# Reordering the opening of a fused Fourier-mixing and hardswish kernel: where raw weights wait, when the second stage starts, who sums x

## The chip, the cores and the metric

The kernel runs on one core of one Trainium2 chip. The metric is the device time of the whole kernel in microseconds (us); before the change its median over three runs is 2004.42 us. The engines are named as in the profile: PE is TensorE (PEld its weight loads), DVE is VectorE, ACT is ScalarE, POOL is GpSimd and SP is SyncE, which here only issues transfers.

## The reference

The first part takes the real part of a two-dimensional Fourier transform of x, over the 3008 sequence positions and the 256 features, for each of 8 batch entries. The result, as 24064 tokens of 256 features, goes through two matrix products with a hardswish between them.

```python
def _attn_ref(x):                      # x: (8, 3008, 256) float32
    X = np.fft.fft(x, axis=1)
    X = np.fft.fft(X, axis=2)
    return X.real.astype(np.float32)

def _moe_ref(x, w_in, w_out):          # x: (24064, 256); w_in: (256, 2048); w_out: (2048, 256), both float64
    h = x @ w_in
    relu6 = np.clip(h + 3.0, 0.0, 6.0)
    g = h * relu6 / 6.0
    return (g @ w_out).astype(np.float32)
```

Both weights are float64: they arrive as 8-byte words and the kernel makes float32 of them itself.

## The kernel before: the opening

The sequence transform is split as 3008 = 47 x 64. Batch entries are taken in four pairs. For the first pair, x arrives in eight parts (`c`); each part is folded (mirrored halves summed) and multiplied by the stage-one table F; the result z goes to DRAM and comes back rearranged as g, on which stage two works with the table T. The feature transform is folded into the weights: `fold_w_in` multiplies w_in by the matrix C. Then come the steps: `mlp1` is the first matrix product with its hardswish, `combine` sums gated values on GpSimd, and `mlp2` is the second product in seven terms instead of eight. There are 384 such steps. Only the opening, up to the first steps, is touched by the change.

The weights come in 16 raw pieces of 512 KB. Pieces 0 to 3 and 6 to 9 belong to w_in, 4, 5 and 10 to 15 to w_out. A piece passes through five operations:

```python
def load_w(j):                                   # GpSimd requests the transfer
    st = wpool.tile([P, 2 * WB], I32, tag="st", bufs=4, name="st")
    ...                                          # nc.gpsimd.dma_start(...)
def exponent_a(j):                               # ScalarE, two passes (L457)
    for i in range(2):
        nc.scalar.activation(low, top, AF.Identity, bias=bias[:, i:i + 1], ...)
def exponent_b(j):                               # TensorE, two matmuls (L462)
    ex = ps_h.tile([P, WB], F32, tag="uv", name="ex")
    ...
def exponent_c(j):                               # ScalarE (L466)
    nc.scalar.activation(exs[j][:].bitcast(I32), exs[j][:], AF.Identity, scale=2.0 ** 23)
def mantissa(j):                                 # VectorE (L474, L475)
    ...
def join(j):                                     # VectorE: mantissa times exponent (L483 or L490)
    ...
```

Two pieces make a pair. A pair of w_in goes through `fold_w_in` (eight TensorE matmuls, L522, into two banks, which ScalarE copies to W1); a pair of w_out goes through `mix_w_out` (four VectorE sums, L509 to L512). The order is set by three functions, in which each engine does its part of piece j and finishes the piece before it:

```python
pending, copies = [], []

def on_scalar(j):
    for i in pending:
        exponent_c(i)
    if j is not None:
        exponent_a(j)
    while copies:
        copies.pop(0)()

def on_vector(j):
    if j is not None:
        mantissa(j)
    for i in pending:
        join(i)

def on_tensor(j):
    if j is not None:
        exponent_b(j)
    done = pending.pop() if pending else 0
    if done % 2:
        use_pair(done // 2)                      # fold_w_in or mix_w_out
    if j is not None:
        pending.append(j)

for c in range(NXC):                             # the eight parts of x
    if c + 2 < NXC:
        load_x(first, c + 2)
    load_w(c + 2)
    if c < NXC - 1:
        fold_first(first, c)                     # half the sums on VectorE, half by accumulation on TensorE
    else:
        for part in range(2):
            fold(first, c, part, nc.vector)      # all sums on VectorE
    on_scalar(c)
    on_vector(c)
    for i in range(XC // 2):
        (stage1_first if c < NXC - 1 else stage1)(first, c, i)
    on_tensor(c)
    if c == 0:
        load_t(0)
    ...
load_g(first, 0)
for j in range(NXC, 15):
    if j < 14:
        load_w(j + 2)
    on_scalar(j)
    on_vector(j)
    keep_awake(1)                                # idle matmuls
    on_tensor(j)
...
keep_awake(2)
for i in range(2):
    stage2(first, 0, i)
spread(first, 0)
...
on_scalar(15)
on_vector(15)
mlp1(*chunk(0))
mlp1(*chunk(1))
on_tensor(15)
combine(*chunk(0))
```

Tiles take their space from pools by tag: `a` (4 buffers) and `c` (3) serve the steps later, and parts of x of the first pair lie in them during the opening. The PSUM tag `uv` has three buffers, shared by `ex`, the idle matmuls and the two halves u and v of `mlp1`. `stage1_first` runs 16 matmul instructions for one part of x, `stage1` half of that work.

Of the kernel before, what the change touches and what calls it, by code (L numbers as in the profile page):

```python
# [8 lines left out]
I32 = mybir.dt.int32  # L9
# [47 lines left out]
def kernel(  # L57
# [10 lines left out]
    nc = tc.nc  # L68
    P = nc.NUM_PARTITIONS
    B, S, D = x.shape  # L70
# [7 lines left out]
    NXC = NS // XC  # L78
# [15 lines left out]
    apool = ctx.enter_context(tc.tile_pool(name="apool", bufs=4))  # L94
    cpool = ctx.enter_context(tc.tile_pool(name="cpool", bufs=3))
# [15 lines left out]
    C = consts.tile([P, 2, D], F32, name="C")  # L111
# [96 lines left out]
    def bank(shape, name):  # L208
        if starting[0]:
            return ps_a.tile(shape, F32, tag="acc", name=name)  # L210
        return ps_d.tile(shape, F32, tag="d", name=name)
# [73 lines left out]
    def spread(pr, gr):  # L285
        pr.qn[gr] = qpool.tile([P, 2 * TB], F32, tag="qn", name="qn")
        if starting[0]:
            ps = bank([P, 2 * TB], "ps3")
            for kk in range(2 * KK):
                nc.tensor.matmul(ps[:, kk * P:(kk + 1) * P], pr.g[gr][:, kk, D:D + 1].to_broadcast([P, P]),  # L290
                                 T[:, :, gr, 1, kk], start=True, stop=True)
            nc.scalar.copy(pr.qn[gr][:], ps[:])
        else:
            qd = dpool.tile([1, 2 * TB], F32, tag="qd", name="qd")
            nc.sync.dma_start(out=qd[:], in_=pr.q[gr][P - 1:P, 1].rearrange("p k n -> p (k n)"))
            nc.sync.dma_start(out=pr.qn[gr][:], in_=qd[:].to_broadcast([P, 2 * TB]))
        del pr.g[gr]
# [120 lines left out]
    first = pairs[0]  # L418

    wctx = tc.tile_pool(name="wpool", bufs=1)  # L420
    wpool = wctx.__enter__()
# [5 lines left out]
    WB = 512  # L427
# [4 lines left out]

    def load_w(j):
        kind, n, i = PIECES[j]
        st = wpool.tile([P, 2 * WB], I32, tag="st", bufs=4, name="st")
        o = st[:].bitcast(moe_w_in.dtype)
        if kind == "in":
            nc.gpsimd.dma_start(out=o, in_=moe_w_in[i * P:(i + 1) * P, n * WB:(n + 1) * WB])
        else:
            r = (2 * n + i * NF) * P  # L440
            nc.gpsimd.dma_start(out=o.rearrange("p (c j) -> p c j", c=2),
                                in_=moe_w_out[r:r + 2 * P, :].rearrange("(c p) d -> p c d", p=P))
        raw[j] = st
# [9 lines left out]
    def exponent_a(j):  # L453
        top = raw[j][:].bitcast(I16).rearrange("p (n four) -> p n four", four=4)[:, :, 3]
        for i in range(2):
            low = PM[:, j % 2, i].bitcast(U8).rearrange("p (n two) -> p n two", two=2)[:, :, 0]
            nc.scalar.activation(low, top, AF.Identity, bias=bias[:, i:i + 1], scale=(1 - 2 * i) / 16.0)  # L457
# [7 lines left out]
    def exponent_c(j):  # L465
        nc.scalar.activation(exs[j][:].bitcast(I32), exs[j][:], AF.Identity, scale=2.0 ** 23)  # L466

    def mantissa(j):
        st = raw.pop(j)
        hi = st[:].rearrange("p (n two) -> p n two", two=2)[:, :, 1]  # L470
        lo = st[:].bitcast(U32).rearrange("p (n two) -> p n two", two=2)[:, :, 0]
        top = wpool.tile([P, WB], I32, tag="top", bufs=2, name="top")
        frac = top[:].bitcast(F32)
        nc.vector.tensor_scalar(top[:], hi, 0xFFFFF, 0x100000, op0=AL.bitwise_and, op1=AL.bitwise_or)  # L474
        nc.vector.scalar_tensor_tensor(frac, lo, 2.0 ** -32, top[:], op0=AL.mult, op1=AL.add)  # L475
        fracs[j] = frac
# [20 lines left out]
    def use_pair(j):  # L497
        kind, n, _ = PIECES[2 * j]
        if kind == "in":
            fold_w_in(n)  # L500
        else:
            mix_w_out(n)
# [11 lines left out]
    def fold_w_in(n):  # L514

        cs = slice(n * WB, (n + 1) * WB)
        ws = [w.pop(("in", n, i)) for i in range(2)]
        sums = []
        for blk in range(2):
            ps = bank([P, WB], "wps")  # L520
            for i in range(2):
                nc.tensor.matmul(ps[:], C[:, i, blk * P:(blk + 1) * P], ws[i], start=(i == 0), stop=(i == 1))  # L522
            sums.append(ps)

        def copy():
            for blk in range(2):
                nc.scalar.copy(W1[:, blk, cs], sums[blk][:])
            nc.sync.dma_start(out=wn[n:n + 1], in_=W1[P - 1:P, 1, cs])

        copies.append(copy)  # L530


    def load_wn(n):
# [3 lines left out]
    def load_t(gr):  # L537
        for b in range(2):
            nc.sync.dma_start(out=T[b * N2:(b + 1) * N2, b, gr], in_=c_stage2[:, gr])


    def keep_awake(n):
        ps = ps_h.tile([P, 2 * TB], F32, tag="uv", name="awake")
        for i in range(n):
            nc.tensor.matmul(ps[:], ones[:], Z[:], start=True, stop=True)
# [1 line left out]
    Z = spool.tile([P, 2 * TB], F32, tag="s", name="Z")  # L547
    nc.vector.memset(Z[:], 0.0)
    nc.vector.memset(ones[:], 1.0)
    keep_awake(6)  # L550
    nc.sync.dma_start(out=F[:], in_=c_stage1)
    bias = wpool.tile([P, 2], F32, tag="bias", name="bias")
    for i in range(2):
# [6 lines left out]
    CE = spool.tile([P, 2, P], F32, tag="s", name="CE")  # L560
    dim = c_dim.rearrange("(h p) d -> p h d", p=P)
    nc.sync.dma_start(out=CE[:], in_=dim[:, :, D:])
    nc.sync.dma_start(out=C[:], in_=dim[:, :, 0:D])
    E = wpool.tile([P, 2, P], F16, tag="E", name="E")
    nc.scalar.copy(E[:], CE[:])
    for b in range(2):
        r = slice((1 - b) * N2, (2 - b) * N2)
        t = T[r, b].rearrange("p g a k n -> p g (a k n)")
# [6 lines left out]
    load_w(0)  # L575
    load_x(first, 1)
    load_w(1)

    pending, copies = [], []

    def on_scalar(j):
        for i in pending:
            exponent_c(i)
        if j is not None:
            exponent_a(j)
        while copies:
            copies.pop(0)()

    def on_vector(j):
        if j is not None:
# [9 lines that stand above are left out]
            use_pair(done // 2)  # L602
        if j is not None:
            pending.append(j)

    for c in range(NXC):
        if c + 2 < NXC:
            load_x(first, c + 2)
        load_w(c + 2)
        if c < NXC - 1:  # L610
            fold_first(first, c)
        else:
            for part in range(2):
                fold(first, c, part, nc.vector)
        on_scalar(c)
        on_vector(c)
        for i in range(XC // 2):
            (stage1_first if c < NXC - 1 else stage1)(first, c, i)
        on_tensor(c)
        if c == 0:  # L620
            load_t(0)
        if c in (4, 6):
            load_wn(PIECES[c - 4][1])
    load_g(first, 0)
    for j in range(NXC, 15):
        if j < 14:
            load_w(j + 2)
        on_scalar(j)
        on_vector(j)
        keep_awake(1)  # L630
        on_tensor(j)
    load_wn(PIECES[6][1])
    load_wn(PIECES[8][1])
    load_g(first, 1)
# [2 lines left out]
    for i in range(2):  # L637
        stage2(first, 0, i)
    spread(first, 0)
    starting[0] = False  # L640


# [3 lines left out]
    after = {}  # L646

    def beside(p):
        at = {}

        def put(t, f, *a):
            at.setdefault(t, []).append((f, a))

        cur = pairs[p]
        if p == 0:
            for f in (on_scalar, on_vector, on_tensor):
                after.setdefault(1, []).append((f, (None,)))
            for gr in range(2, NG):
                after.setdefault(gr, []).append((load_t, (gr,)))
            put(NF - 1, close_w)  # L660

        def s2(t, pr, gr):
            for i in range(2):
                put(t + 3 + 4 * i, stage2, pr, gr, i)
            put(t + 8, spread, pr, gr)

        for gr in range(1, NG):
            if gr > 1:
                put(NST * (gr - 2) + 12, load_g, cur, gr)
            s2(NST * (gr - 1), cur, gr)  # L670
        if p + 1 < NP:
            nx = pairs[p + 1]
            for c in range(NXC):
                put(9 * c, load_x, nx, c)
                put(9 * c + 3, fold, nx, c, 0, nc.gpsimd)
                put(9 * c + 5, fold, nx, c, 1, nc.gpsimd)
                for i in range(XC // 2):
                    put(9 * c + 8 + 3 * i, stage1, nx, c, i)
            put(NST * (NG - 1) - 2, load_g, nx, 0)
            put(NST * (NG - 1) + 8, load_g, nx, 1)  # L680
            s2(NST * (NG - 1), nx, 0)
        return at
# [10 lines left out]
    def chunk(s):  # L693
        p, ck, fc = steps[s]
        return chunks[p][ck], fc

    on_scalar(15)
    on_vector(15)
    mlp1(*chunk(0))
    mlp1(*chunk(1))  # L700
    on_tensor(15)
    combine(*chunk(0))
    prev = None
    for s, (p, ck, fc) in enumerate(steps):
# [96 lines left out]
```

## Time and profile before

| | before |
|---|---|
| median of three runs | 2004.42 us (2000.66 to 2004.54) |
| span of the profiled run, mean granted TensorE clock | 2002.9 us, 0.993 |
| busy: PE, DVE, ACT, POOL | 1965.6, 1437.2, 701.2, 1417.9 us |
| first 82 us: PE, DVE, ACT, POOL busy | 72.0, 45.7, 52.5, 23.4 us |
| first 82 us: DMA share, moved | 0.93, 256 GB/s |

How to read it: the busy times say how long an engine had work, not whether it set the end. A line of the chain gives the start, the duration and what ran. A line of the order of time gives start, duration, engine, line of the kernel, operation, output and input, with the idle time before it and what ended that in brackets. A line of the waits says which group waited for which: us in total, times, longest.

### The profile page before, as it was taken

The page shows a single profiled execution, that of the slowest core. Times are in us where ns is not written, and L with a number is a line of the kernel's source. Part 1 is how long each engine was busy: PE and PEld are TensorE (multiplying, and loading weights), DVE is VectorE, ACT ScalarE, POOL GpSimd, SP SyncE. Part 2 cuts the span into 40 slices and gives each one's busy share as a digit, 9 for nine tenths or more (in the row PEclk, how much of TensorE's full clock was granted, in tenths as well). Part 3 has the DMA queues.
Part 4 walks back from the last instruction along what each step waited for, and adds up shares of the span by engine and source line. Part 5 has one row for each costly group of instructions (what it writes and reads, how often), then busy time and mean ns, then how long its engine had stood idle before and what let it go on. Part 6 is the DMA issues. An engine that isn't in the chain of part 4 may idle for free.

```text
span 2002.9 us, 28366 instructions
## 1 busy us (share of the span) xinstructions
PE 1965.6 (98%) x9178; PEld 1691.5 (84%) x9178; DVE 1437.2 (72%) x2701; ACT 701.2 (35%) x1198; POOL 1417.9 (71%) x1612
## 2 busy tenths in 40 slices
PE   9899999999999999999999999999999999999997
PEld 5488888888888888888888888888888888888886
DVE  5677767776777777776777767777678777777775
ACT  6533333333333333333333333333333333333332
POOL 3277778776777787777658877778666667667665
PEclk9899999999999999999999999999999999999998
DMA  9512211211112122110201221112110101101100
GB/s 275 162 27 59 51 40 48 55 38 35 28 35 51 41 51 56 50 51 25 48 18 30 69 56 39 51 43 53 35 27 20 27 17 27 32 12 27 27 11 19
DMA packets 158985, 93.54 MB, mean 47 GB/s; under 512 B 131019, under 2 KB 143819, under 8 KB 158838
## 3 DMA queue, kind: packets, MB, share of 16 engines
q1 hardware_dynamic: 149366, 58.22, 12.1%
q0 software_dynamic: 9472, 33.49, 6.1%
q8 instruction: 75, 1.23, 0.3%
q14 instruction: 72, 0.59, 0.1%
HBM read 54.32 MB, written 37.33 MB: 46 GB/s over the span
## 4 chain that ended last, share of the span: by engine, by line
PE 93%; DVE 3%; ACT 1%; issue 0%; POOL 0%; DVEq 0%; POOLq 0%; ACTq 0%
PE acc L379 55%; PE v L325 16%; PE u L325 16%; PE ps L280 2%; PE ps L226 2%; DVE a L357 1%; ACT t L354 0%; DVE u L338 0%; DVE s L330 0%; ACT PM L457 0%; PE wps L522 0%; DVE o L405 0%; DVE v L344 0%; DVE u L341 0%; PE ps L223 0%
## 5 line engine op out<-in xcount | busy, mean ns | idle before, releaser
L369 POOL TENSOR_TENSOR c<-a 128x512 f32<-128x512 f32 (+1 forms) x384 | 478.4, 1246 | 454.9 <-PE acc L379 358.1
L379 PE MATMUL acc<-c,G 128*128 128x256 f32 (+1 forms) x3072 | 712.1, 375 | 0.0
L354 ACT ACTIVATE t<-u,half 128x512 f32<-128x512 f32 (+2 forms) x416 | 272.4, 655 | 1104.6 <-DVE u L338 1092.9
L379 PEld LDWEIGHTS acc<-c,G 128*128 128x128 f32 x3072 | 577.5, 190 | 72.7
L330 DVE SCALAR_TENSOR_TENSOR s<-qn,WN,u 128x256 f32<-128x256 f32 x768 | 334.6, 477 | 351.6 <-PE u L325 351.2
L379 PE MATMUL acc<-a,G 128*128 128x256 f32 (+1 forms) x2304 | 551.2, 375 | 0.0
L379 PEld LDWEIGHTS acc<-a,G 128*128 128x128 f32 x2304 | 434.6, 190 | 57.6
L325 PE MATMUL v<-q,W 127*128 127x256 f32 x1536 | 397.7, 381 | 7.7 <-DVE a L357 7.7
L325 PE MATMUL u<-q,W 128*128 128x256 f32 x1536 | 395.4, 380 | 2.5 <-DVE a L357 2.2
L325 PEld LDWEIGHTS u<-q,W 128*128 128x128 f32 x1536 | 287.8, 190 | 59.9 <-issue 15.8
L325 PEld LDWEIGHTS v<-q,W 127*128 127x128 f32 x1536 | 289.7, 190 | 55.6 <-issue 8.2
L357 DVE SCALAR_TENSOR_TENSOR a<-t,u 128x512 f32<-128x512 f32 (+2 forms) x416 | 266.1, 646 | 95.7 <-ACT t L354 90.3
L369 POOL TENSOR_TENSOR c<-c,a 128x256 f32<-128x256 f32 (+1 forms) x384 | 274.7, 715 | 30.1
L369 POOL TENSOR_TENSOR c<-a,c 128x256 f32<-128x256 f32 (+1 forms) x384 | 274.6, 715 | 30.1
L338 DVE TENSOR_TENSOR u<-s,v 128x512 f32<-128x512 f32 (+1 forms) x384 | 263.1, 685 | 41.5 <-DVE s L330 0.9
L354 ACT ACTIVATE t<-v,half 128x512 f32<-128x512 f32 (+1 forms) x384 | 257.1, 670 | 5.8 <-DVE v L344 4.5
L344 DVE TENSOR_TENSOR v<-v,s 128x512 f32<-128x512 f32 (+1 forms) x384 | 257.9, 672 | 1.1
L357 DVE SCALAR_TENSOR_TENSOR a<-t,v 128x512 f32<-128x512 f32 (+1 forms) x416 | 255.4, 620 | 0.5
L369 POOL TENSOR_TENSOR r<-w,e 128x256 f32<-128x256 f32 (+1 forms) x96 | 92.2, 981 | 3.8
L385 ACT ACTIVATE e<-acc 128x512 f32<-128x512 f32 (+1 forms) x192 | 87.0, 543 | 2.9 <-PE acc L379 2.8
L405 DVE STREAM_TRANSPOSE o<-r 128x256 f32<-128x256 f32 (+1 forms) x192 | 72.5, 416 | 6.6 <-POOL r L369 6.4
L238 ACT COPY z<-ps 96x512 f32<-96x512 f32 x64 | 37.2, 581 | 83.5 <-PE ps L226 63.1
(81 smaller groups left out, 754.0 us busy)
## 6 DMA issues: line engine op xcount, KB each, us to landing
out_dram<-o SPq DMA_DIRECT2D x736, 32.0 KB
zd<-z SPq DMA_DIRECT2D x32, 384.0 KB
g<-zd SPq DMA_DIRECT2D x48, 256.0 KB
xt<-in_x_dram POOLq DMA_DIRECT2D x21, 384.0 KB, 4.0
qn<-qd SPq DMA_DIRECT2D x23, 256.0 KB
st<-in_moe_w_in_dram POOLq DMA_DIRECT2D x8, 512.0 KB, 11.8
st<-in_moe_w_out_dram POOLq DMA_DIRECT2D x8, 512.0 KB, 5.7
xt<-in_x_dram POOLq DMA_DIRECT2D x7, 376.0 KB, 3.9
```

The costliest lines, as they stand in the source:

```text
L226: nc.tensor.matmul(ps[0:PZ], F[0:PR, 0:PZ], y[:, 2 * i:2 * i + 2, :], start=True, stop=True)
L280: nc.tensor.matmul(ps[:, blk, 2 * u:2 * u + 2], g[:, kk, blk * (P + 1):blk * (P + 1) + P], T[:, :, gr, blk, kk], start=True, stop=True)
L325: nc.tensor.matmul(ps[:, i], W1[r, blk, f * P:(f + 1) * P], q[r, blk, of:of + KC], start=True, stop=True)
L330: nc.vector.scalar_tensor_tensor(s[:, i].rearrange("p k n -> p (k n)"), qn[:, of * N2:(of + KC) * N2], WN[:, f:f + 1], u[:, i].rearrange(" ...
L338: nc.vector.tensor_tensor(u[:, :, 0:ns], s[:, :, 0:ns], v[:, :, 0:ns], op=AL.add)
L344: nc.vector.tensor_tensor(v[:, :, 0:nm], v[:, :, 0:nm], s[:, :, 0:nm], op=AL.subtract)
L354: nc.scalar.activation(t, h, AF.Relu, bias=half[:], scale=scale)
L357: nc.vector.scalar_tensor_tensor(dst, t, 1.0, h, op0=AL.min, op1=AL.mult)
L369: nc.gpsimd.tensor_tensor(out, in0, in1, op=AL.add)
L379: nc.tensor.matmul(ch.acc[i // 2][:, i % 2, 0:ch.n], G[:, i, fc, :], mv, start=(fc == 0 and i % 2 == 0), stop=(fc == NF - 1), skip_group_c ...
L385: nc.scalar.mul(ch.e[:, k:i + 1, 0:ch.n], ch.acc[i // 2][:, 0:i + 1 - k, 0:ch.n], 1.0 / WS)
L405: nc.vector.transpose(o[:, 0:n // DH, h], ch.r[:, m, h, 0:n].rearrange("p (j i) -> p j i", i=DH))
```

## The change

Five things are moved in the opening; what is computed stays the same.

- Raw pieces 8 to 14 are put into buffers of the pools `a` and `c`, which x has left by then, so that their requests need not wait for the conversion of earlier pieces. All requests are made by the last part of x, behind x itself.
- Parts 2 and 4 of x are summed wholly on VectorE, like the last one, which takes accumulating matmuls from TensorE in the parts where it also does `fold_w_in`.
- On ScalarE the first exponent pass of piece j comes before the last one of piece j-1, and the copies of a folded pair are taken one piece later, so that ScalarE doesn't stand waiting for TensorE.
- Stage two and the spread stand behind piece 12 instead of 14; pieces 13 to 15 are finished between stage two and the first steps.
- The tables C and T are requested later, and the opening has two more idle matmul calls.

```diff
     def load_w(j):
         kind, n, i = PIECES[j]
-        st = wpool.tile([P, 2 * WB], I32, tag="st", bufs=4, name="st")
+
+        pool, tag = (wpool, "st") if j < 8 or j == 15 else (apool, "a") if j < 12 else (cpool, "c")
+        st = pool.tile([P, 2 * WB], I32, tag=tag, bufs=4 if pool is wpool else None, name="st")
...
-        copies.append(copy)
+        copies[-1].append(copy)
...
-    keep_awake(6)
+    keep_awake(8)
...
-    nc.sync.dma_start(out=C[:], in_=dim[:, :, 0:D])
...
-    pending, copies = [], []
+    pending, copies = [], [[], []]

     def on_scalar(j):
+        for copy in copies.pop(0):
+            copy()
+        copies.append([])
+        if j is not None:
+            exponent_a(j)
         for i in pending:
             exponent_c(i)
-        if j is not None:
-            exponent_a(j)
-        while copies:
-            copies.pop(0)()
...
-        load_w(c + 2)
-        if c < NXC - 1:
+        for j in [c + 2] if c < NXC - 2 else range(4 * c - 16, 4 * c - 12):
+            load_w(j)
+        on_pe = c not in (2, 4, NXC - 1)
+        if on_pe:
             fold_first(first, c)
         else:
             for part in range(2):
...
-            (stage1_first if c < NXC - 1 else stage1)(first, c, i)
+            (stage1_first if on_pe else stage1)(first, c, i)
         on_tensor(c)
         if c == 0:
+            nc.sync.dma_start(out=C[:], in_=dim[:, :, 0:D])
+        if c == 3:
             load_t(0)
...
-    for j in range(NXC, 15):
-        if j < 14:
-            load_w(j + 2)
+    for j in range(NXC, 13):
         on_scalar(j)
         on_vector(j)
+        on_tensor(j)
         keep_awake(1)
-        on_tensor(j)
...
     spread(first, 0)
+    on_scalar(13)
+    on_vector(13)
+    on_tensor(13)
     starting[0] = False
...
         if p == 0:
-            for f in (on_scalar, on_vector, on_tensor):
-                after.setdefault(1, []).append((f, (None,)))
+            for t, f, j in ((0, on_scalar, 15), (0, on_vector, 15), (1, on_tensor, 15),
+                            (2, on_scalar, None), (2, on_vector, None), (2, on_tensor, None)):
+                after.setdefault(t, []).append((f, (j,)))
...
-    on_scalar(15)
-    on_vector(15)
+    on_scalar(14)
+    on_vector(14)
     mlp1(*chunk(0))
+    on_tensor(14)
     mlp1(*chunk(1))
-    on_tensor(15)
     combine(*chunk(0))
```

## The prediction

> **What bounds the kernel now.** I read the busy times by stage first, since every edit lies in the opening, then the chain of work that ended last for the opening, then the waits, then the order of time around the last part of x. The stages (us, busy time and number of instructions of each engine, TensorE clock, DMA share, GB/s):
>
> ```profile
> 0.00:82.00 82.00, 72.02 (x244) 41.16 (x245) 45.74 (x101) 52.47 (x85) 23.41 (x37) 0.94 0.93 256
> 82.00:112.00 30.00, 24.06 (x103) 19.53 (x102) 23.92 (x41) 9.32 (x15) 16.32 (x17) 0.89 0.11 31
> 112.00:1990.00 1878.00, 1869.48 (x8835) 1630.79 (x8833) 1366.56 (x2557) 639.23 (x1099) 1375.04 (x1555) 1.00 0.15 38
> ```
>
> From 112 us on TensorE is busy 1869.5 of 1878 us: nothing the diff touches is there, and whatever the opening gains or loses moves the end one for one. The prize is bounded too: the first output matmuls (L379) start at 93.67 us in the order of time, so 2% (40 us) would be nearly half of all that precedes them.
>
> The chain between the last stage-one matmuls and the first hidden layer (start, duration, what):
>
> ```profile
> 58.06 3.43 PE wps L522 x8
> 61.49 0.86 PE awake L545 x2
> 62.35 0.45 PE ex L462 x2
> ...
> 63.31 1.41 ACT PM L457 x2
> ...
> 64.77 0.38 PE ex L462
> 65.14 3.43 PE wps L522 x8
> ...
> 76.97 1.72 PE awake L545 x4
> 78.69 1.78 PE ps L280 x16
> 80.47 0.91 PE ps L290 x8
> ```
>
> No DMA stands in it: ScalarE's two exponent passes (PM, 1.41) and TensorE's weight products (wps, 3.43) hand over to each other, about 7.1 us per pair of w_in pieces. The requests for raw weights do wait for their buffers, in the waits of the opening:
>
> ```profile
> POOL st L441 <- ACT PM L457: 15.5, 5, 5.0
> ```
>
> but this is GpSimd's own idle time; pieces 8 to 15 are converted without a single wait for a transfer. While x comes in it is otherwise: VectorE waits for it. Order of time around piece 6 and the last part of x:
>
> ```profile
> 45.77 0.57 ACT L466 ACTIVATE ex<-ex 128x512 int32<-128x512 f32 x1
> 46.06 0.43 DVE L474 TENSOR_SCALAR top<-st 128x512 int32<-128x512 int32 x1 [1.21 <-DMA st<-in_moe_w_in_dram]
> 46.28 1.41 ACT L457 ACTIVATE PM<-st,bias 128x512 uint8<-128x512 int16 x2
> ...
> 47.13 0.75 DVE L490 TENSOR_TENSOR G<-top,ex 128x256 f32<-128x256 f32 x2
> 47.79 0.42 DVE L509 TENSOR_TENSOR G<-G,b 128x256 f32<-128x256 f32 x1
> ...
> 49.38 0.55 DVE L165 TENSOR_TENSOR xt<-xt 94x381 f32<-94x381 f32 x1
> ```
>
> Piece 6 lands at 46.06 us, piece 5 is joined at 47.13, its four sums follow from 47.79, and at 49.38 the fold of the last x starts with no idle time before it. So the landing of piece 6 and VectorE's order set when x is done.
>
> **What the Trainium skill says.** "TensorE: Matmul & The Clock Gate", Part 1: activity is watched in windows of about 3.4 us, an idle one halves the clock. The trace agrees in kind and is harsher: after 2.45 us of idling at 9.16 us the matmuls run at the low clock until about 19.8 us. "DMA: Bandwidth & Descriptors", Queues, rings and completion order: each engine goes round the queues that have work, so weights queued on GpSimd can share time with the writes and reads of z from SyncE; the DMA share of 0.93 over the first 82 us fits, the sharing itself no view shows apart. "GPSIMD Engine Reference", 1. Specifications: VectorE instructions with two SBUF inputs contend with GpSimd. Here the sums of a w_out pair take 0.42 us at 71 us with GpSimd idle, and 0.83 to 1.48 us at 103 to 106 us beside its additions.
>
> **The change part by part.** I lay the new order out with the durations above.
>
> *Buffers and requests.* Pieces 8 to 14 need no longer wait for the conversion of 4 to 10. In the trace pieces 10 to 15 were requested at 47.98, 54.00, 57.93, 60.30, 65.02 and 67.38 us; now all should be out soon after 50. The traffic stays; at the 200 to 300 GB/s of that stretch the last of them (4.2 MB for eight) should land about 67 us, instead of about 73 (67.38 plus the 5.7 of a w_out piece). As nothing on the chain waited for them: 0 us. C behind the first part of x and T behind the fourth move 0.26 MB each about within a stretch in which the DMA engines are full: x arrives some 1 us earlier at first and the same by piece 6: 0 us.
>
> *Two parts of x on VectorE.* It costs 2 x (2 x 0.55 + 0.68 + 0.68 + 0.16 - 1.52) = 2 x 1.1 us of VectorE and saves TensorE half of 3.4 us twice. TensorE did lag by 3 us in the fourth part (x folded at 27, its products from 30.1), but had caught up by the seventh (folded 44.85, products from 45.18). 0 us. Two more keep-awake matmuls fill the gap before 11.6 us; x binds there: 0 us.
>
> *ScalarE's order.* exponent_a(j) now comes before exponent_c(j-1). For piece 6 this hurts: exponent_a waits for the landing at 46.06 and takes 1.42, exponent_c 0.58, so the join of piece 5 starts at 48.1, not 47.13; with the sums the fold of the last x starts about 50.5, not 49.38: **+1.1 us**. Afterwards exponent_a(8) from 56.8, exponent_c(7) to 58.8, join (0.69) to 59.5: the first late wps at 59.5 instead of 57.9, another **+0.5**. From the end of one wps block to the start of the next: copy 0.58 + exponent_a 1.42 + exponent_c 0.58 + join 0.69 + hand-overs 0.25 = 3.5 us; before it was 64.98 - 61.49 = 3.5. The looser order gains nothing there, since the copies now stand ahead of exponent_a.
>
> *Second stage behind piece 12.* From the start of the second wps to stage two: wps 3.43 + copy 0.59 + exponent_a 1.42 + ex 0.4 + three keep-awakes 2.6 + hand-overs 0.2 = 8.6 us; before 78.69 - 64.98 = 13.7: **-5.1**. Stage two starts about 75.1 and the spread row is copied by 78.4 (before 81.98). But two pieces now stand between it and the first hidden layer: exponent_a(13) 1.42, exponent_c(12) 0.58, exponent_a(14) 1.42, exponent_c(13) 0.58, join 0.75 = 4.75 us, where before it took 83.18 - 81.98 = 1.2: **+3.55**. The first s (L330) thus starts at 83.15, as before (83.18).
>
> *Sums in the first steps.* The four sums of the third w_out pair, 4 x 0.42 = 1.7 us, now stand on VectorE between the first and the second mlp1, where TensorE has nothing else and waits for a bank: **+1.65**. Piece 15 moves from before the first mlp1 to steps 0 to 2: 1.1 + 0.75 us and then a join and sums beside GpSimd, about 4 us. VectorE has some 1.15 us to spare per 4.75 us step, and a similar backlog cost 1.55 us at 110 us before: 0.
>
> Sum: +1.1 + 0.5 - 5.1 + 3.55 + 1.65 = **+1.7 us**, so the first mlp2 at about 95.4 us instead of 93.67.
>
> **The rivals.** (a) The weights really were late and the conversion runs ahead: stage two at 70 us, the end at 1996 to 1999. The 15.5 us of waiting requests speak for it; that no conversion after piece 7 waited for a transfer speaks against. (b) The clock. No keep-awake now stands between ex(7) and ex(8), so TensorE has a gap of some 1.4 us after 4 us of idling, and part of the eight wps matmuls may run at the low clock: +1 to +2, 2006 to 2008. (c) With eight weight transfers queued, z of the last part and the rows g for stage two land late. Before, g was requested at 60.4, three us after the last z request; it has until 75 us, and only past that does the end move: 2007 to 2012. The margin of about 5 us speaks against.
>
> **Range and chances.** The laid-out sum gives 2006.1. I shade it by one microsecond to 2005.0: the order of short operations on ScalarE can fall better than I laid it, and the three runs of before reach from 2000.66 to 2004.54 with the median at the top. Each of five terms is uncertain by 1 to 2 us, so 3 to 4 together; with the rivals and the 4 us of spread: 1998 to 2011. More than 40 us either way is out of reach of an opening of 94 us with this DMA traffic: 0.01 faster, 0.98 the same, 0.01 slower.
>
> **What would show it.** Right: the last x folded on VectorE near 50.5; wps blocks near 59.5 and 66.5; stage two (L280) near 75; the first s near 83; four sums of 0.42 between the first two groups of s; the first L379 near 95; no DMA in the chain after 55 us. Wrong: conversion of pieces 8 to 12 ahead of 55 us or faster than 6.9 us per pair, stage two before 72 us, a wait of L280 for g, or a main stage whose 8.5 us of TensorE idling has changed.

## The result, and the profile after

The changed kernel takes 2012.04 us (2011.36 to 2012.93, four runs), the kernel before 2004.47: a ratio of 1.0043, with a 95% interval of 1.0025 to 1.006. That is within 2%, as forecast, but 7.6 us longer by the medians (8.6 by the ratio), outside the range of 1998 to 2011 us and far above the 0.6 us that the 2005.0 amounts to.

The stages of the changed kernel (columns as before: us, busy time and instructions of PE, PEld, DVE, ACT and POOL, TensorE clock, DMA share, GB/s):

```profile
0.00:82.00 82.00, 67.20 (x212) 35.48 (x213) 42.61 (x93) 47.51 (x78) 23.99 (x37) 0.94 0.80 247
82.00:112.00 30.00, 22.16 (x78) 16.79 (x78) 23.52 (x41) 10.85 (x18) 12.20 (x13) 0.77 0.20 56
112.00:1990.00 1878.00, 1869.03 (x8828) 1629.84 (x8827) 1370.69 (x2562) 638.01 (x1096) 1375.61 (x1554) 1.00 0.15 38
```

The main stage is untouched: 1869.0 us of TensorE against 1869.5. The difference lies in the opening, where TensorE has done less work by 82 us (67.2 us against 72.0). A sharper measure is the start of the output products of the fifth step: 115.87 us before, 122.98 us after. From there to the end of the span it is 1887.0 us before (2002.9 - 115.87) and 1886.6 after (2009.6 - 122.98), and between 1886.6 and 1887.0 in every trace of this study. So each traced execution can be judged by that one instant.

The chain of the changed kernel from the last part of x on (start, duration, what):

```profile
54.81 0.46 DVE xt L165
...
63.89 3.67 PE wps L524 x8
...
70.14 3.45 PE wps L524 x8
...
78.88 1.78 PE ps L280 x16
```

Compare with the chain before: stage two (L280) at 78.88 against 78.69, though it now stands behind piece 12 and not 14. What the new order saves has been lost ahead of it: the last part of x is folded from 54.7 us, not 49.4. And between the last weight product and stage two, 5 us shorter as predicted, the chain still has no transfer. The transfer that hurts is earlier. The order of time around the first weight product, TensorE and SyncE:

```profile
16.40 0.58 SPq L625 DMA_DIRECT2D C<-in_c_dim_dram  x1
...
22.73 0.60 PE L464 MATMUL ex<-PM,E 128*128 128x512 f16 x2
...
27.84 6.74 PE L524 MATMUL wps<-wi,C 128*128 128x512 f32 x8 [4.51 <-DMA C<-in_c_dim_dram]
...
34.41 0.60 PE L199 MATMUL ps<-xt,F 94*96 94x258 f32 x2
```

C is requested at 16.40 us and the first product that needs it starts at 27.84, after 4.51 us in which TensorE stood still; the products of the fourth part of x, which was folded at 22.4 us, stand behind it in TensorE's program. Behind the gap the eight matmuls take 6.74 us, and from 28 to 32 us the granted clock is 0.50. In the kernel before, the same line in the order of time has no wait and takes 3.60:

```profile
26.69 3.60 PE L522 MATMUL wps<-wi,C 128*128 128x512 f32 x8
```

So TensorE loses 4.51 + 3.14 = 7.65 us there, and the fourth part of x is multiplied only from 34.41.

The start of landmarks in us, in the two profiles (s is VectorE's first result in an mlp1, L330; the value predicted for the second s follows from its 83.15 and its +1.65):

| | before | after | predicted for after |
|---|---|---|---|
| last x folded (L165) | 49.38 | 54.73 | 50.5 |
| first late weight product | 57.90 | 63.73 | 59.5 |
| second late weight product | 64.98 | 69.98 | 66.5 |
| stage two | 78.53 | 78.72 | 75.1 |
| first s | 83.18 | 86.51 | 83.15 |
| second s | 86.87 | 93.67 | 88.5 |
| first output product | 93.67 | 100.46 | 95.4 |
| output products of the fifth step | 115.87 | 122.98 | - |

Stage by stage the change is +5.35 (to the last fold), +0.48, -0.83, -4.81 (to stage two), +3.14 (to the first s), +3.47 (to the second), -0.01, +0.32: together 7.11 us. Two of these need a cause that the prediction didn't have: the first and the one between the first and the second s.

### The profile page after: what moved, and what is told of

It reads as the page before. It is cut to its first block, busy times and chain, and to the rows that moved or that the text cites. A ratio compares the mean times of both kernels' runs of the same rounds, so it can differ in the third digit from the quotient of the medians.

```text
span 2009.6 us, 28311 instructions
## 1 busy us (share of the span) xinstructions
PE 1964.8 (98%) x9154; PEld 1688.3 (84%) x9154; DVE 1440.3 (72%) x2705; ACT 699.5 (35%) x1198; POOL 1418.8 (71%) x1612
## 4 chain that ended last, share of the span: by engine, by line
PE 92%; DVE 3%; ACT 1%; issue 0%; SPq 0%; DMA 0%; POOL 0%; DVEq 0%; POOLq 0%; ACTq 0%
PE acc L379 55%; PE v L325 16%; PE u L325 16%; PE ps L280 2%; PE ps L226 2%; DVE a L357 1%; ACT t L354 0%; DVE u L338 0%; DVE s L330 0%; PE wps L524 0%; DVE o L405 0%; PE awake L547 0%; SPq L411 0%; DMA out_dram<-o 0%; PE ps L223 0%
## 5 line engine op out<-in xcount | busy, mean ns | idle before, releaser
L330 DVE SCALAR_TENSOR_TENSOR s<-qn,WN,u 128x256 f32<-128x256 f32 x768 | 334.3, 477 | 350.7 <-PE u L325 350.1
```

The costliest lines, as they stand in the source:

```text
L330: nc.vector.scalar_tensor_tensor(s[:, i].rearrange("p k n -> p (k n)"), qn[:, of * N2:(of + KC) * N2], WN[:, f:f + 1], u[:, i].rearrange(" ...
```

## The experiments

Theory: C comes too late, and TensorE carries the loss through the parts of x. Rival: the new order on ScalarE and VectorE makes the last fold late, and C's wait is absorbed. A second question is the sums between the first two mlp1.

Each ratio compares a run with the kernel before on the same chip; it is estimated with its interval and is not the quotient of two medians. Medians of different rows can come from different chips, on which the kernel before itself had medians of 2003.9 to 2005.5 us. Single executions of one kernel spread over up to 10 us here. A trace, and with it the landmarks of a row, is one execution: those of e1, e12 and e9 are 2.7, 2.9 and 4.0 us faster than the medians beside them, those of e5 and e6 2.8 and 4.3 us slower. So the lengths of stages inside a trace are better evidence than its instants.

| run | median us | ratio to before (95%) | last fold | stage two | first s | second s | fifth step |
|---|---|---|---|---|---|---|---|
| after (first timing) | 2012.04 | 1.0043 (1.0025 to 1.006) | 54.73 | 78.72 | 86.51 | 93.67 | 122.98 |
| after_again | 2012.25 | 1.0039 (1.0025 to 1.0053) | 54.21 | 80.21 | 88.00 | 95.16 | 124.46 |
| e1_c_early | 2007.49 | 1.0014 (1.0003 to 1.0024) | 47.49 | 72.08 | 79.87 | 87.03 | 116.34 |
| e12_c_early_again | 2009.39 | 1.0020 (1.001 to 1.003) | 49.25 | 73.84 | 81.63 | 88.79 | 118.09 |
| e2_tables_early | 2008.59 | 1.0019 (1.0011 to 1.0027) | 49.44 | 74.04 | 81.84 | 88.99 | 118.32 |
| e3_before_c_late | 2007.22 | 1.0011 (1.0005 to 1.0018) | 52.97 | 81.59 | 86.25 | 89.93 | 119.47 |
| e4_sums_later | 2011.39 | 1.0032 (1.002 to 1.0045) | 54.94 | 80.98 | 88.77 | 92.45 | 123.74 |
| e5_c_early_sums_later | 2005.68 | 1.0008 (1.0002 to 1.0015) | 52.64 | 77.22 | 85.01 | 88.70 | 119.99 |
| e6_c_early_scalar_old | 2007.53 | 1.0013 (1.0006 to 1.002) | 49.74 | 79.46 | 86.47 | 94.03 | 123.34 |
| e7_c_early_stage_late | 2007.15 | 1.0015 (1.0009 to 1.0022) | 49.01 | 78.04 | 83.99 | 87.68 | 117.91 |
| e8_c_early_buffers_old | 2007.86 | 1.0025 (1.0012 to 1.0037) | 49.04 | 75.56 | 83.34 | 90.50 | 119.61 |
| e9_early13 | 2005.13 | 1.0005 (0.9999 to 1.0012) | 47.51 | 71.44 | 75.69 | 82.06 | 112.45 |
| e10_c_early_fold_pe | 2007.47 | 1.0012 (1.0004 to 1.0019) | 51.24 | 75.83 | 83.63 | 90.79 | 119.71 |
| e11_best | 2002.06 | 0.9988 (0.9979 to 0.9997) | 48.08 | 71.28 | 75.53 | 81.90 | 112.30 |

**C back at its old place.**

```diff
     nc.sync.dma_start(out=CE[:], in_=dim[:, :, D:])
+    nc.sync.dma_start(out=C[:], in_=dim[:, :, 0:D])
...
-        if c == 0:
-            nc.sync.dma_start(out=C[:], in_=dim[:, :, 0:D])
```

> The changed kernel with the request of C back at its old place, before x. Theory (late C): in the changed kernel the first weight product waits 4.5 us for C and then runs 6.7 instead of 3.6 us at a low clock, and TensorE carries these 8 us on to the last part of x. Then here the first weight product starts near 23.5 us and takes about 3.6, the fold of the last part of x starts near 47 instead of 54.7 us, and the whole takes 2003 to 2006 us. Rival (order on ScalarE and VectorE): the last fold is late because exponent_a stands before exponent_c and two parts of x are summed on VectorE; C's wait is absorbed. Then the last fold stays at 53 us or later and the whole at 2010 or more.

Order of time of this run, TensorE:

```profile
23.72 3.60 PE L524 MATMUL wps<-wi,C 128*128 128x512 f32 x8
```

The wait is gone, the product takes 3.60 us, the last fold starts 7.2 us earlier, at 47.49, and the fifth step 6.6 us. The theory's landmarks came as told (23.5, 3.6, 47). The time, 1.0014 of before, was 1.5 us above the upper end expected. Because the two had been timed on different chips, both ran once more side by side:

> The changed kernel once more, beside the version with C early, on one chip. Theory (late C): its first weight product again waits 4 to 5 us for C and runs at the low clock, whatever the arrival of x; its time lies 4 to 6 us above the version with C early. Rival (the difference seen so far came from the arrival of x and the clock, which change from run to run): less than 2 us apart.

> The changed kernel with C back at its old place, once more, beside the changed kernel on one chip. Theory (late C): 4 to 6 us below the changed kernel and 1 to 3 us above the kernel before, which is what the prediction's sum gave without the wait for C. Rival: less than 2 us below the changed kernel.

The changed kernel again shows the gap and the low clock:

```profile
27.96 6.08 PE L524 MATMUL wps<-wi,C 128*128 128x512 f32 x8 [4.33 <-DMA C<-in_c_dim_dram]
```

The medians differ by 2.9 us, the ratios by 0.0019 (3.8 us), the two traces by 6.4 us in the span. Of the 6.4, 3.6 come from where the two traced executions lie beside their medians (2.9 us below and 0.6 above). The time thus falls just short of the 4 to 6 us expected here, and the rival's less than 2 doesn't fit. With the first pair of timings, whose ratios differ by 0.0029 (5.8 us), C's wait is worth 3 to 6 us of the loss; with C early the rest, 3 to 4 us over the kernel before, stays.

**Both tables back.** As above, and `load_t(0)` again behind the first part of x.

> The changed kernel with both tables at their old places: C before x, T behind the first part of x. Theory (late C): C explains the loss, so the time is that of the run with C alone moved back, 2003 to 2006, within 1.5 us of it. Rival (T in the way of x): T early delays x by some 3 to 5 us, as the kernel before shows it against the changed one (fifth part of x at 32.0 against 26.9 us); then this is 2 to 5 us slower than with C alone moved back.

1.1 us above e1_c_early in the median, with overlapping intervals: the times can't be told apart. In the trace x was later (fifth part at 31.0 against 28.5 us), as the rival had it, and the last fold later by 1.95 us; e12, with T late, has its last fold at 49.25 as well, so this one trace doesn't settle T.

**C late in the kernel before.**

```diff
         if c == 0:
+            nc.sync.dma_start(out=C[:], in_=dim[:, :, 0:D])
             load_t(0)
```

(and the request ahead of x taken out)

> The kernel before with one thing of the change alone: C is requested behind the z of the first part of x, together with T. Theory (late C): C lands some 11 us after its request near 18 us, so the first weight product waits from 26.5 to about 29.5 us and may then run at the low clock; the whole takes 2007 to 2011 us. Rival: the kernel before has slack there, and stays within 1.5 us of 2004.5.

```profile
27.97 6.65 PE L522 MATMUL wps<-wi,C 128*128 128x512 f32 x8 [4.60 <-DMA C<-in_c_dim_dram]
```

The same wait and the same slow product appear in the old order, and the last fold moves from 49.4 to 53.0 us. The late request of C is thus enough for both, without the new order. The cost in time is 1.8 us by the medians and 2.2 by the ratio: the theory's 2007 to 2011 meant 2.5 us or more over its 2004.5, so the cost lies between theory and rival, and below the 3 to 6 us that C is worth in the new order.

**The sums behind the second mlp1.**

```diff
     mlp1(*chunk(0))
-    on_tensor(14)
     mlp1(*chunk(1))
+    on_tensor(14)
```

> The changed kernel with piece 14's exponent matmuls and the four sums of the third w_out pair behind the second mlp1 instead of between the first and the second. Theory (sums on the path): the four sums took 3.5 us there, beside GpSimd, and the second group of s waited for them; now it starts about 3.3 us earlier, near 90.3 us, and the whole takes 2008 to 2009.5 us. Rival: the sums only move on, into the start of the third mlp1, and as much is lost there; the whole stays at 2011 or more.

First what is moved: in the changed kernel the order of time between the first two groups of s reads, on VectorE and GpSimd,

```profile
86.51 0.87 DVE L330 SCALAR_TENSOR_TENSOR s<-qn,WN,u 128x256 f32<-128x256 f32 x2
90.19 0.42 DVE L511 TENSOR_TENSOR G<-G,b 128x256 f32<-128x256 f32 x1
90.36 1.37 POOL L369 TENSOR_TENSOR c<-a 128x512 f32<-128x512 f32 x1 [40.31 <-DVE a L357]
90.65 1.37 DVE L512 TENSOR_TENSOR G<-G 128x256 f32<-128x256 f32 x1
91.81 0.79 POOL L369 TENSOR_TENSOR c<-c,a 128x256 f32<-128x256 f32 x1
92.05 0.83 DVE L513 TENSOR_TENSOR G<-G 128x256 f32<-128x256 f32 x1
...
92.80 0.94 DVE L514 TENSOR_TENSOR G<-G,b 128x256 f32<-128x256 f32 x1
93.67 0.86 DVE L330 SCALAR_TENSOR_TENSOR s<-qn,WN,u 128x256 f32<-128x256 f32 x2
```

The first sum runs alone and takes 0.42 us. Then GpSimd begins the first `combine`, and the other three take 1.37, 0.83 and 0.94: 3.5 us from the first sum to the second s, not 1.7. In e4_sums_later the same view shows where they went:

```profile
88.77 0.86 DVE L330 SCALAR_TENSOR_TENSOR s<-qn,WN,u 128x256 f32<-128x256 f32 x2
92.45 0.87 DVE L330 SCALAR_TENSOR_TENSOR s<-qn,WN,u 128x256 f32<-128x256 f32 x2
96.65 0.42 DVE L511 TENSOR_TENSOR G<-G,b 128x256 f32<-128x256 f32 x1
97.11 1.74 DVE L512 TENSOR_TENSOR G<-G 128x256 f32<-128x256 f32 x1
...
100.50 0.86 DVE L330 SCALAR_TENSOR_TENSOR s<-qn,WN,u 128x256 f32<-128x256 f32 x2
```

The second s follows the first by 3.68 instead of 7.16 us, but the third follows the second by 8.05 instead of 5.33. From stage two to the fifth step it is 42.8 us here and 44.3 in the changed kernel: 1.5 us of the 3.5 stay, the rest is moved into the next step. Stage two itself came later in this trace (a weight product ran at the low clock for 5.67 us), so its instants are read against it. The median, 2011.39, lies where the rival put it (2011 or more) and not at the theory's 2008 to 2009.5; the interval is too wide to tell 1.5 us from none. The same edit with C early:

> C back at its old place, and piece 14's matmuls and the four sums of the third w_out pair behind the second mlp1. Theory (VectorE carries the first steps): against C early alone the second s comes 3.4 us earlier and the first output product (93.8 us there) 3 us earlier, but the sums then stand before the third s and two thirds of it are lost again: the fifth step's output products start near 115 instead of 116.3 us, and the whole is 0.5 to 2 us shorter. Rival (the sums are the whole remaining loss): all of it stays, the fifth step starts near 113, the whole is 3 to 3.5 us shorter.

From stage two to the fifth step 42.8 us, against 44.3 in e1_c_early: again 1.5 us. The second s wins 3.5 us on the first, the third loses 2.7 of it. The ratio is 0.0006 (1.2 us) below e1, about what the theory said, though the intervals overlap. In this trace the last fold and stage two were late by 5 us, so its fifth step is not the expected 115.

**Stage two again behind piece 14, C early.** The tail of the old order: pieces 13 and 14 ahead of stage two, piece 15 behind.

> C back at its old place, and the second stage again behind piece 14, with piece 15 as in the kernel before. Theory (what stage two gains is given back behind it): stage two starts 5 to 6 us later than with C early alone (72.1 us), but the first s at 80 to 81 and the second only 3.7 us behind it, so the fifth step's output products start near 114.3 instead of 116.3 us, and the whole is 1 to 3 us shorter. Rival (an early stage two helps): the whole is 2 us or more longer.

Second late weight product 64.86, stage two 78.04, first s 83.99, second s 3.69 us behind. From that product to the first s it takes 19.1 us here and 16.5 in e1_c_early; from the first s to the fifth step 33.9 here and 36.5 there. The early stage two gains 2.6 us and gives back 2.6. So neither side is borne out: the new place is worth nothing in all, where the theory had it cost 1 to 3 us and the rival had it gain 2; the ratios, 1.0015 and 1.0014, say the same.

**Old buffers, C early.**

> C back at its old place, and raw pieces in the old four buffers with the old places of the requests. Theory (hidden anyway): the conversion never waited for pieces 8 to 15, so nothing is lost but what x, now earlier, leaves open: last fold within 1 us of 47.5, the whole within 1.5 us of C early alone. Rival (requests at once are what keeps the conversion fed): waits for transfers appear in the conversion of pieces 10 to 13, stage two is 3 us or more later, the whole 3 us or more longer.

Raw pieces are again requested up to 69.3 us, and in the trace no conversion waits for a transfer. Against e12, which has the same last fold (49.25 and 49.04), stage two is 1.7 us later, and all of that is one weight product that ran at the low clock (5.59 against 3.83 us). In the trace the buffers are hidden, as predicted. The ratio (1.0025) lies 1.0 and 2.2 us above those of e12 and e1 with overlapping intervals, so the time alone doesn't exclude a cost of that size.

**ScalarE's old order, C early.**

> C back at its old place, and ScalarE's old order: exponent_c of the piece before, then exponent_a, then the copies at once. Theory (the prediction's term): exponent_a first costs about 1 us at piece 6, so the last fold here starts near 46.4 instead of 47.5 us; the weight products then follow each other at 7.1 us as in the kernel before instead of 6.25 as with C early alone, so this is given back, and the whole is within 1.5 us of C early alone. Rival (the looser order is a gain): the fifth step's output products start at 118.5 us or later (116.3 with C early alone).

The ratio is that of e1_c_early (1.0013 and 1.0014). The instants of this trace don't decide: x came late in it (fifth part at 31.8 us) and a weight product took 6.18 us at the low clock. The join of piece 5, ahead of the last fold, does show the term. First e1_c_early, then this run:

```profile
45.23 0.75 DVE L492 TENSOR_TENSOR G<-top,ex 128x256 f32<-128x256 f32 x2 [2.14 <-ACT ex L468]
...
46.44 0.74 DVE L492 TENSOR_TENSOR G<-top,ex 128x256 f32<-128x256 f32 x2
...
49.74 0.55 DVE L165 TENSOR_TENSOR xt<-xt 94x381 f32<-94x381 f32 x1 [0.97 <-DMA xt<-in_x_dram,IX]
```

With the new order VectorE stands 2.14 us in front of this join, because the copies of the pair before (1.04 us) and exponent_a (1.42) now come ahead of exponent_c; with the old one it doesn't wait. From ScalarE's last operation for z (L253) to the join it is 3.08 us in e1, 3.06 to 3.08 in eight more traces with the new order, and 1.05 here. About 1 us of what is gained went to a wait for x itself in this trace. The weight products then follow each other at 9.67 us, or 7.1 without the 2.6 of the slow one, against 6.24 in e1: what the order costs in front of the last fold it partly wins back there, the theory's direction.

**Half of the sums again on TensorE in all parts of x but the last, C early.** `on_pe = c < NXC - 1`.

> C back at its old place, and parts 2 and 4 of x again half summed by TensorE's accumulation. Theory (not on the path): TensorE has 3.4 us more work but no idle stretch and no low clock between 12 and 47 us; the last fold starts within 1 us of 47.5 us unless x itself comes later, and the whole is within 1.5 us of C early alone. Rival (TensorE binds the x loop): the last fold starts at 50 us or later, the whole is 3 us or more longer.

The ratio, 1.0012, is again close to that of e1. In the trace x was late (fifth part 32.6 us) and the last fold at 51.2; TensorE's clock was full between 12 and 47 us, but so it was in e1 (0.95 in e12). Which way x is summed makes no difference that these runs show.

**The kernel before again.**

> The kernel before once more, for a second trace of it. If x's arrival differs from run to run, the fifth part of x is folded up to 3 us away from 32.05 us and the fifth step's output products move by less; if the traces of the kernel before agree within 0.5 us in both, the earlier arrival of x in the changed kernel comes from the change itself.

Fifth part of x at 31.81 us, fifth step at 116.05, span 2003.0: both traces of the kernel before agree within 0.5 us, which by the expectation makes the early x an effect of the change. But over all traces with C ahead of x and T behind the fourth part, the fifth part of x was folded near 28.5 us six times and near 32 three times; with C late always by 28.5 (four times). The three late ones are late from the first part on (folded at 10.4 to 10.7 us against 9.0 to 9.6 in the six). This isn't explained; it is one reason why executions spread.

Another is the first late weight product. In the 13 traces with the new order on TensorE it took 3.83 us eight times and 4.9 to 6.2 us five times, each of these with a granted clock of 0.50 in its first 2 us; in the three traces with the old order it took 3.59. That is rival (b) of the prediction, and it can be part of the 3 to 4 us that stay with C early.

**A version that beats both.** First, piece 13 taken by ScalarE and VectorE ahead of stage two, while TensorE runs keep-awake matmuls, the first mlp1 right behind the spread, piece 14 behind it and the sums behind the second mlp1:

```diff
+    on_scalar(13)
+    on_vector(13)
     keep_awake(2)
     for i in range(2):
         stage2(first, 0, i)
     spread(first, 0)
-    on_scalar(13)
-    on_vector(13)
     on_tensor(13)
...
-    on_scalar(14)
-    on_vector(14)
     mlp1(*chunk(0))
-    on_tensor(14)
+    on_scalar(14)
+    on_vector(14)
     mlp1(*chunk(1))
+    on_tensor(14)
```

> C back at its old place; ScalarE and VectorE take piece 13 before stage two, while TensorE is in its keep-awake matmuls; the first mlp1 follows the spread at once, piece 14 stands between the first and the second mlp1, the four sums behind the second. Theory (the wait behind stage two is only the order on ScalarE): first s near 75.5 instead of 79.9 us, second near 81 instead of 87, first output product near 88 instead of 93.8; VectorE's work is only moved, so about half of that is lost by the fifth step (near 113 instead of 116.3), and the whole is 2 to 5 us shorter than with C early alone, below the kernel before. Rival (VectorE's total work binds): fifth step at 115.5 or later, the whole within 1 us of C early alone.

The landmarks came nearly as told: first s 75.69, second 82.06, first output product 88.57, fifth step 112.45. But this trace is the fastest of 21 executions. What doesn't depend on that: from stage two to the first s it is 4.25 us instead of 7.8, and to the fifth step 41.0 instead of 44.3. In time it is level with the kernel before and, by the ratios, 1.8 us below e1, just short of the 2 to 5 us expected. Then, added to it, half of the sums on TensorE in all parts of x but the last, exponent_a ahead of the copies, and keep-awake matmuls only behind pieces without a weight product:

> A version meant to beat both: C early, all parts of x but the last half summed on TensorE, piece 13 before stage two on ScalarE and VectorE, first mlp1 right behind the spread, the sums behind the second mlp1, exponent_a ahead of the copies, and keep-awake matmuls only behind pieces without a weight product. Expected from the run with piece 13 early (fifth step's output products at 112.4 us): one microsecond less at each of the two late weight products, so the fifth step near 110.5 us and the whole 3 to 5 us below the kernel before. If VectorE's total work binds the first steps, the fifth step stays at 112 or later, 1 to 3 us below it.

Order of time of this run:

```profile
57.91 4.94 PE L524 MATMUL wps<-wi,C 128*128 128x512 f32 x8
```

2002.06 us, 0.9988 of the kernel before (0.9979 to 0.9997): 2.4 us shorter, less than the 3 to 5 hoped for, 3.4 us below e9 by the ratios and some 10 us below the changed kernel. The fifth step, at 112.30, stands where it does in e9's trace, but that one is exceptionally fast. From stage two to the fifth step it is 41.0 us in both. Ahead of it the second late product is followed by stage two after 6.87 us instead of 8.74; the first late product, the line above, began 0.9 us further behind the last fold and took 4.94 us at the low clock instead of 3.83. So the gain lies at one of the two weight products and was partly lost at the other; that VectorE's work binds the first steps is not shown by this, and what each of the three additions is worth was not separated.

## Why the prediction was wrong

**The step that failed** is in "Buffers and requests": "C behind the first part of x and T behind the fourth move 0.26 MB each about within a stretch in which the DMA engines are full: x arrives some 1 us earlier at first and the same by piece 6: 0 us." It priced C only as traffic in the way of x and never asked when C itself is needed. The trace before had all that was wanted: the z of the first part, behind which C now stands, was requested at 18.27 us, the first weight product ran at 26.69, and the transfers of x and of weights in the first 30 us took 11 to 15 us (medians by kind) from request to landing. That gives, as an estimate from transfers of GpSimd's queue, a landing at 29 to 33 us, late for the first product. Measured: requested at 16.40, used at 27.84. The gap then cost the clock as well, so the wait of 4.5 us became 7.7. e1 and e12 against the changed kernel and e3 against the kernel before show it, from both sides; it is worth 3 to 6 us of the 7.6.

**A term mis-sized.** The sums between the first two mlp1 were put at 4 x 0.42 = 1.65 us; they took 3.47, for GpSimd's first combine starts the moment the first hidden layer is done. The prediction named this contention and had its numbers (0.83 to 1.48 us), but used them for the later sums only. With 1.8 us more, the sum without C is about +3.5, where the two timings with C early show 2.8 and 4.0 us by the ratios. Part of this agreement is luck: e4 and e5 show that only 1.5 us of the sums' place is felt at the fifth step, and other terms are off in both directions (below).

**What held.** Weights requested at once: 0 us in the trace of e8. x summed on VectorE: no difference in time (e10). From the second weight product to stage two -4.81 against -5.1, and to the first s +3.14 against +3.55; e7 shows that the new place of stage two is worth nothing in all. The first weight product behind the fold +0.48 against +0.5, though with C early it is +1.1 (9.6 us in e1 and e12 against 8.5).

**Off in size.** ScalarE's order at piece 6, put at +1.1 us, holds VectorE for 2.1 us in front of the join in e1: the copies of the pair before were left out of the sum. The interval between the late weight products was 6.25 us, not the 7.0 laid out: the second product begins with piece 8 alone, joined at 65.8, while the join of piece 9 (70.00) runs beside it, so exponent_c and that join don't stand in its way. For the sums of a part of x wholly on VectorE two instructions were put at 0.55 us that take 0.68 on a full part. And the low clock behind the gap at 9.16 us was read as beginning too early: the first matmuls there still took 0.59 to 0.68 us, and the granted clock is 0.69 from 12 to 14 us and 0.50 from 14 to 18.

**Not settled.** I had x the same by piece 6; in the changed kernel its fifth part came 5 us earlier (3.6 in the second trace), which the late C hid, and why it comes early in some runs is open. T's place was tried only in e2, which doesn't settle it, and the two added idle matmuls were not tested by themselves.

Of the rivals named beforehand, (a) and (c) did not come. (b), part of the weight product at the low clock, came in five traces of thirteen. None was a transfer moved later by the change itself.

## What to carry to other kernels

When a request is moved later to make room, work out its own deadline: the time of the first use minus the time from request to landing that transfers of that same stretch show, not its size over the bandwidth. A wait on TensorE should be counted with the slow matmuls behind it. And work that is moved from one engine's stretch to another should be priced at what it costs beside its new neighbours; here three sums went from 0.42 to between 0.83 and 1.37 us. And before two traces are compared instant by instant, it should be asked how fast each execution was among its like.

## What was unexpected of the hardware

A transfer of 256 KB, requested from SyncE while transfers of GpSimd's queue took 92% of the DMA engines' time (10 to 26 us of the changed kernel), was usable only 11.4 us later. After gaps of 4.3 to 4.7 us eight matmuls took 6.1 to 6.7 us instead of 3.6, in all four traces with C late. And the same opening varies by several us between runs with nothing changed: x's fifth part near 28.5 or near 32 us, and the first late weight product now 3.8, now 4.9 to 6.2 us, the longer ones at a granted clock of 0.50.
